# Queries and keys stored by quad and head column, and packed by fewer transfers

## The chip, the core and the metric

The kernel runs on one core of a Trainium2 chip. The metric is the device time of one execution in microseconds; the figure given for a kernel is the median of its runs. Five engines work side by side: PE (TensorE, matrix products), DVE (VectorE), ACT (ScalarE), POOL (GpSimd), and SP (SyncE), which in this kernel issues every DMA transfer. Each engine executes its own instructions strictly in the order in which the program has them; an instruction that waits on a semaphore holds up everything behind it on that engine.

## The reference, cut to what matters

Input `x` is 2048 rows of 640 numbers. Four layers follow one another, each added to its input:

```python
x = x + _A_ref(_layernorm(x))   # attention
x = x + _B_ref(_layernorm(x))   # Fourier mixing
x = x + _A_ref(_layernorm(x))
x = x + _B_ref(_layernorm(x))
```

`_A_ref` makes q, k and v by one 640 x 1920 product, splits them into 32 heads of 20 numbers, takes `q @ k.T * 20 ** -0.5` where the key lies 0 to 255 places behind the query, a softmax over the keys, the product with v, and an output product with a 640 x 640 matrix. `_B_ref` is a two-dimensional DFT by matrix products, of which the real part is kept. Only the two attention layers are touched here.

## The kernel before, in words

Everything is float32. A product of two float32 matrices is made of three products of their halves: a matrix is cut into a rounded upper part ("hi") and the remainder ("lo"), and hi·hi + hi·lo + lo·hi is summed in PSUM (`split` L171, `product3` L182). This holds for q·k too, which matters for the change.

**Projection.** Queries and keys come out transposed, with the feature on the partition and the sequence along the row, in 10 chunks of 128 features by 4 blocks ("sb") of 512 positions. The host has put the columns of the weight in an order in which 160 features in a row belong to one quad (four heads): first 80 of the query, then 80 of the key, and head after head inside these. 160 and 128 don't divide each other, so most chunks hold features of two quads. `piece` (L495) makes one chunk and sb, and `store_qk` (L503) writes hi and lo into the DRAM tensor `qk_d` by one transfer. That is for the first two chunks, before the heads begin; the other eight come from `pieces` (L507) while the heads run, whose `store` (L531) writes hi and lo by a transfer each (L533).

**Heads.** `heads` (L575) is one software pipeline over 128 steps, 16 steps (query blocks of 128) for each of 8 quads. In step `step` the score pass runs for s = step + 10 and the exponent pass for t = step, so that the score pass is 10 steps ahead (`LEAD`):

- score pass (`s_head`, matmul L606): scores of a query block, and on DVE (L611) the mask and the row maximum. Contraction is over 60 partitions: 20 rows of the head three times, queries as hi, lo, hi and keys as hi, hi, lo, so that one matmul makes the three products.
- after every 4 steps `m_rows` (L615) turns the maxima of 512 queries round on PE, ACT writes them negated to the tile `mt` (L622), and two small transfers (L624) put them into partitions 60 and 124 of the query tile `qp`, opposite a row of ones in the key tile `kp`.
- exponent pass (`t_head`, matmul L638): keys against queries over 61 partitions, which subtracts the maximum as well; exponent on ACT (L649), mask on POOL (L655, L659), and the product with v on PE (`pv`, L672).

The first exponent matmul that touches a block's queries needs that block's `mt` rows. For blocks 1 to 3 of a quad it stands a little under three steps behind ACT's write of `mt`; for block 0 two steps more.

**Packing.** `pack` (L557) brings the tiles `kp` and `qp` of a quad from `qk_d`, one block of 512 positions at a time: 20 partitions by two heads by 512 numbers for each of 3 groups of rows, for 2 head pairs, for keys and for queries, so 12 transfers of 80 KB a block (L563). `due` (L710) asks for a block 8 steps before its first use, every 4 steps, and `defer(i // 3, f)` spreads the 12 transfers over four steps, 3 a step. Two sets of `kp` and `qp` alternate by quad.

**Order of the transfers.** All of these stand in SP's one queue in the order in which the Python code reaches them: the packs by step (`defer`), the stores and the small transfers of sums by half step (`post`, `tick`), the loads of v every 4 steps (`load_v` L588), and loads for the output product and the next layer in the last quads. Each transfer counts on one of eight semaphores in turn, and its issue waits until the transfer eight places before it has landed.

Projection matmuls (L204) and later parts of the output product are laid between the heads' matmuls by `share` and `fill` (L740, L757), in numbers fixed when the program is built.

## Time and profile before

| | |
|---|---|
| median of 3 runs | 2169.74 us (2169.26 to 2172.96) |
| profiled execution | 2169.5 us, of which the span of its instructions 2167.7 us |
| PE, DVE, ACT, POOL busy | 97%, 74%, 53%, 43% of the span |
| mean granted PE clock | 0.992 |
| DMA | 222400 packets and 392.26 MB through SP's queue, mean 182 GB/s |
| pack transfers (L563) | 2 x 384 of 80.0 KB |
| heads, first to last exponent matmul | 154.6 to 517 us and 1236.0 to 1595 us |

How to read it: a line such as L638 is a line of the kernel printed above. "PE banks L638 <- DMA qp<-mt" says that PE's matmul of line 638, which writes the tile `banks`, waited for the transfer that wrote `qp` from `mt`. The chain is the path of work that ended last, followed back from the last instruction. Windows give each engine's busy time in a stretch of the span, then the granted PE clock (1.00 is full), the busy share of the 16 DMA engines, and the rate. In a timeline a row is: start, duration, engine ("SPq": SP issuing a transfer), line, operation, tiles, count, and in brackets the idle time before it and what ended that.

### The profile page before, as it was taken

Reading aid. Unit: us, or ns where it says so; the run is one execution under the profiler, and the core shown is the slowest. Engines: PE = TensorE matmul, PEld = TensorE weight load, DVE = VectorE, ACT = ScalarE, POOL = GpSimd, SP = SyncE. Lnnn points to the kernel's source line nnn. Section 1 sums busy time; section 2 is a strip of 40 time slices with the busy share of each in tenths; the row PEclk is TensorE's granted clock in tenths of the full one; section 3 lists DMA queues with packets and bytes.
Section 4 is the critical chain, followed back from the end, with each engine's and each line's share of the span. In section 5 each row is a group of like instructions: output and inputs, shape, how many; then the busy total and the mean of one; then the engine's idle time right before and its main releaser. Section 6 shows DMA issues by size and latency. Waiting matters only on the chain.

```text
span 2167.7 us, 46148 instructions
## 1 busy us (share of the span) xinstructions
PE 2108.8 (97%) x16405; PEld 1749.2 (81%) x16405; DVE 1596.9 (74%) x3936; ACT 1153.9 (53%) x2511; POOL 925.3 (43%) x1455
## 2 busy tenths in 40 slices
PE   8999999999999999999999999999999999999999
PEld 8987776677878888889999877766777788888899
DVE  7358777676897968777751578876778869687777
ACT  3228877666554545543431288776665545455522
POOL 2047776766423234130230487777654323241300
PEclk9999999999999999999999999999999999999999
DMA  6556666786445454757645466667864464546653
GB/s 210 169 162 184 202 191 207 206 229 199 140 125 178 134 180 127 230 193 259 213 143 185 152 186 202 200 205 225 230 183 134 126 189 136 165 149 218 221 177 125
DMA packets 222630, 395.21 MB, mean 182 GB/s; under 512 B 40384, under 2 KB 86976, under 8 KB 222400
## 3 DMA queue, kind: packets, MB, share of 16 engines
q1 hardware_dynamic: 222400, 392.26, 58.3%
q8 instruction: 130, 2.13, 0.4%
q14 instruction: 100, 0.82, 0.1%
HBM read 273.94 MB, written 117.05 MB: 180 GB/s over the span
## 4 chain that ended last, share of the span: by engine, by line
PE 78%; DVE 7%; DMA 5%; ACT 4%; POOL 4%; issue 2%; SPq 1%; ACTq 0%; DVEq 0%; POOLq 0%
PE banks L1373 27%; PE banks L186 15%; PE banks L204 12%; PE banks L672 7%; PE banks L1628 6%; PE banks L638 5%; PE banks L606 4%; DMA qp<-mt 3%; POOL big L179 1%; POOL ou L1303 1%; DVE qp L179 1%; PE banks L286 1%; ACT big L1023 1%; DMA pt<-c 1%; POOL rs L1073 1%
## 5 line engine op out<-in xcount | busy, mean ns | idle before, releaser
L611 DVE CUSTOM_DVE_ANT_0 banks<-banks,mask 128x384 f32<-128x384 f32 (+2 forms) x1024 | 515.0, 566 | 175.5 <-PE banks L606 140.1
L649 ACT ACTIVATE pt<-banks 128x384 f32<-128x384 f32 (+2 forms) x864 | 363.0, 472 | 100.9 <-PE banks L638 47.8
L638 PE MATMUL banks<-qp,kp 61*128 61x384 f32 (+2 forms) x1024 | 336.6, 366 | 19.4 <-DMA qp<-mt 18.2
L606 PE MATMUL banks<-kp,qp 60*128 60x384 f32 (+2 forms) x1024 | 337.4, 370 | 5.4 <-DVE mc L611 4.5
L204 PE MATMUL banks<-big,wc 64*128 64x512 f32 x1920 | 338.4, 398 | 0.4 <-DVE pt L419 0.4
L655 POOL TENSOR_SCALAR_AFFINE_SELECT pt<-pt 128x256 f32<-128x256 f32 x432 | 177.4, 412 | 148.6 <-ACT pt L649 123.8
L638 PEld LDWEIGHTS banks<-qp,kp 61*128 61x128 f32 x1024 | 178.7, 187 | 63.6 <-issue 25.2
L606 PEld LDWEIGHTS banks<-kp,qp 60*128 60x128 f32 x1024 | 174.1, 187 | 58.1 <-DVE mc L611 41.9
L204 PEld LDWEIGHTS banks<-big,wc 64*128 64x128 f32 x1920 | 199.1, 188 | 12.3 <-DVE pt L419 0.5
L1303 POOL TENSOR_TENSOR pt<-pt,pt 128x512 f32<-128x512 f32 x36 | 62.9, 1747 | 289.3 <-DMA pt<-c 176.1
L672 PE MATMUL banks<-pt,vq 128*32 128x128 f32 (+1 forms) x3664 | 178.4, 317 | 1.3 <-POOL pt L655 1.2
L173 ACT ACTIVATE cc<-pt 128x512 fp32r<-128x512 f32 x150 | 94.0, 626 | 155.0 <-POOL pt L1279 52.7
L173 ACT ACTIVATE qp<-pt 128x512 fp32r<-128x512 f32 (+1 forms) x195 | 119.6, 624 | 94.2 <-DVE pt L1304 46.4
L179 DVE TENSOR_TENSOR cc<-pt,cc 128x512 fp32r<-128x512 f32 x150 | 120.1, 811 | 53.5 <-ACT cc L173 51.1
L659 POOL TENSOR_SCALAR_AFFINE_SELECT pt<-pt 128x256 f32<-128x256 f32 x380 | 156.6, 412 | 0.0
L1373 PE MATMUL banks<-qp,big 128*128 128x512 f32 x630 | 151.1, 391 | 5.0 <-DVE qp L179 4.0
L179 DVE TENSOR_TENSOR qp<-pt,qp 128x512 fp32r<-128x512 f32 (+1 forms) x195 | 147.6, 770 | 10.4 <-ACT qp L173 7.7
L672 PEld LDWEIGHTS banks<-pt,vq 128*32 128x32 f32 x3664 | 101.3, 111 | 61.0 <-issue 22.7
L611 DVE DVE_READ_ACCUMULATOR2_ANT mc<- 128x1 f32 x1024 | 146.3, 143 | 0.0
L1373 PEld LDWEIGHTS banks<-qp,big 128*128 128x128 f32 x630 | 117.0, 188 | 31.0 <-DVE qp L179 5.7
L1373 PE MATMUL banks<-qp,xc 128*128 128x512 f32 x480 | 118.0, 391 | 2.0 <-DVE xc L179 1.5
L1373 PEld LDWEIGHTS banks<-qp,xc 128*128 128x128 f32 x480 | 89.8, 188 | 22.6 <-DVE xc L179 2.4
(232 smaller groups left out, 4561.5 us busy)
## 6 DMA issues: line engine op xcount, KB each, us to landing
pt<-c SPq DMA_DIRECT2D x188, 512.0 KB
kp<-qk_d SPq DMA_DIRECT2D x384, 80.0 KB
qp<-qk_d SPq DMA_DIRECT2D x384, 80.0 KB
kp<-u_d SPq DMA_DIRECT2D x32, 640.0 KB
qk_d<-cc SPq DMA_DIRECT2D x64, 256.0 KB
qk_d<-x SPq DMA_DIRECT2D x64, 256.0 KB
o_d<-ou SPq DMA_DIRECT2D x64, 256.0 KB
x_d<-x SPq DMA_DIRECT2D x48, 320.0 KB
```

Of the source, the lines that this page charges most:

```text
L173: nc.scalar.activation(hi, src, AF.Copy, scale=-1.0 if neg else 1.0)
L179: (eng or nc.vector).tensor_tensor(out=lo, in0=src, in1=hi.bitcast(F32), op=OP.subtract)
L186: self.nc.tensor.matmul(p, x, y, start=n == 0, stop=n == last)
L204: self.nc.tensor.matmul(ps[a], x[r], y[r], start=half + i == 0, stop=half == 1 and i == n - 1, skip_group_check=True)
L606: nc.tensor.matmul(p, qp[quad % 2][b:b + 60, z, qb * P:(qb + 1) * P], kp[quad % 2][b:b + 60, z, k0 * P:(qb + 1) * P], start=True, stop=True)
L611: nc.vector.tensor_tensor_reduce(out=p, in0=p, in1=self.mask[:, 384 - n * P:], scale=1.0, scalar=NEG, op0=OP.add, op1=OP.max, accum_out=mc ...
L638: nc.tensor.matmul(self.banks[:, tb[e], :n * P], kp[quad % 2][b:b + 61, z, kb * P:(kb + 1) * P], qp[quad % 2][b:b + 61, z, kb * P:(kb + n) ...
L649: nc.scalar.activation(pt[quad, kb][:, 2 * z + e, :n * P], self.banks[:, tb[e], :n * P], AF.Exp, scale=SCALE)
L655: nc.gpsimd.affine_select(out=t[:, :, 0:P], in_=t[:, :, 0:P], pattern=[[0, 2], [1, P]], compare_op=OP.is_ge, fill=0.0, base=0, channel_mul ...
L659: nc.gpsimd.affine_select(out=t[:, :, 256:384], in_=t[:, :, 256:384], pattern=[[0, 2], [-1, P]], compare_op=OP.is_gt, fill=0.0, base=0, ch ...
L672: nc.tensor.matmul(p[32 * h:32 * h + 32, (c0 - qa) * P:(c1 - qa) * P], vq[:, 96 * (kb % 4) + 21 * h:96 * (kb % 4) + 21 * h + 32], t[:, h, ...
L1373: nc.tensor.matmul(self.banks[:, bk, :], p, b[q], start=start and m == 0, stop=stop and last and m == 2, skip_group_check=True)
```

## The change

`qk_d` becomes a tensor by quad, part (hi, lo), feature of the quad, and position, with rows of 2560 numbers instead of 2048 (512 are never used). The host orders the 160 columns of a quad by feature number first, and by query or key and head after that, so that one head's 20 features lie 8 rows apart, and hi and lo of a head are 40 rows with one step between them. Where two neighbouring groups of the 60 partitions are hi and then lo, one transfer of 40 partitions brings both. `pack` so needs 8 transfers instead of 12, and in the heads it takes two blocks (1024 positions) at once, every 8 steps instead of every 4, spread over six steps. A chunk that holds features of two quads is now stored by two sets of transfers.

```diff
-        self.qk = dram.tile([2, 2 * D, S], F32, name="qk_d")
+        self.qk = dram.tile([NQ, 2, 8 * DH, S + 512], F32, name="qk_d")
...
+    def rows_of(self, c):
+        n, r0, r1 = 8 * DH, c * P, (c + 1) * P
+        for q in range(r0 // n, -(-r1 // n)):
+            a, b = max(r0, q * n), min(r1, q * n + n)
+            yield q, a - q * n, a - r0, b - r0
+
     def store_qk(self, c, sb, st):
-        self.nc.sync.dma_start(
-            self.qk[:, c * P:(c + 1) * P, sb * 512:(sb + 1) * 512].rearrange("l p s -> p l s"), st.bitcast(F32))
+        for q, r0, a, b in self.rows_of(c):
+            self.nc.sync.dma_start(
+                self.qk[q, :, r0:r0 + b - a, sb * 512:(sb + 1) * 512].rearrange("l p s -> p l s"),
+                st[a:b].bitcast(F32))
...
             def store():
-                for l, x in enumerate((hi.bitcast(F32), r)):
-                    self.nc.sync.dma_start(self.qk[l, c * P:(c + 1) * P, sb * 512:(sb + 1) * 512], x)
+                for q, r0, a, b in self.rows_of(c):
+                    for l, x in enumerate((hi.bitcast(F32), r)):
+                        self.nc.sync.dma_start(self.qk[q, l, r0:r0 + b - a, sb * 512:(sb + 1) * 512], x[a:b])
...
-    def pack(self, quad, sb):
+    def pack(self, quad, sb, n=1):
...
-        cols = slice(sb * 512, (sb + 1) * 512)
+        cols = slice(sb * 512, (sb + n) * 512)
...
+        src = self.qk[quad].rearrange("l (r g) s -> (l r) g s", g=8)
         for kind in (1, 0):
             for e in range(2):
-                r0 = 160 * quad + 80 * kind + 40 * e
                 dst = (self.qp, self.kp)[kind][quad % 2].rearrange("p (z s) -> p z s", z=2)
-                for part, l in enumerate(((0, 1, 0), (0, 0, 1))[kind]):
-                    b = 64 * e + 20 * part
-                    src = self.qk[l, r0:r0 + 40, cols].rearrange("(z r) s -> r z s", z=2)
-                    todo.append(lambda d=dst[b:b + 20, :, cols], src=src: put(d, src))
+                g = 4 * kind + 2 * e
+                for part, m in (((0, 2), (2, 1)), ((0, 1), (1, 2)))[kind]:
+                    b = 64 * e + DH * part
+                    todo.append(lambda d=dst[b:b + DH * m, :, cols], src=src[:DH * m, g:g + 2, cols]: put(d, src))
...
-               for q in range(1, NQ) for j in range(NSB)]
+               for q in range(1, NQ) for j in range(0, NSB, 2)]
...
-                for i, f in enumerate(self.pack(q, j)):
-                    defer(i // 3, f)
+                for i, f in enumerate(self.pack(q, j, 2)):
+                    defer(3 * i // 4, f)
...
-        for kind in range(2):
-            for e in range(2):
-                for z in range(2):
-                    b = kind * D + (4 * p + 2 * z + e) * DH
-                    cols.extend(range(b, b + DH))
+        for d in range(DH):
+            for kind in range(2):
+                for e in range(2):
+                    for z in range(2):
+                        cols.append(kind * D + (4 * p + 2 * z + e) * DH + d)
```

On PE, DVE, ACT and POOL the instructions stand in the same order as before, one for one. Only SP's queue differs.

First place: SP in the first attention layer, where the first blocks of quad 3 are packed into `kp_103` and `qp_104` while `mt` rows go to quad 2's `qp_105`. Before:

```order
L563 DMA kp_103<-qk_d 20x2x512 x3
L624 DMA qp_105<-mt 2x4x128 x2
L563 DMA kp_103<-qk_d 20x2x512 x3
L701 DMA r_d<-rc 128x16
L533 DMA qk_d<-cc 128x512
L533 DMA qk_d<-x 128x512
L563 DMA qp_104<-qk_d 20x2x512 x3
L590 DMA vq_90<-v_d 128x384
L563 DMA qp_104<-qk_d 20x2x512 x3
```

Now (the pack is line 572, `mt` line 633, the stores line 542):

```order
L572 DMA kp_103<-qk_d 20x2x1024
L572 DMA kp_103<-qk_d 40x2x1024
L633 DMA qp_105<-mt 2x4x128 x2
L572 DMA kp_103<-qk_d 20x2x1024
L710 DMA r_d<-rc 128x16
L542 DMA qk_d<-cc 128x512
L542 DMA qk_d<-x 128x512
L572 DMA kp_103<-qk_d 40x2x1024
L599 DMA vq_90<-v_d 128x384
L572 DMA qp_104<-qk_d 40x2x1024
L572 DMA qp_104<-qk_d 20x2x1024
```

Two transfers of 160 and 320 KB stand ahead of `mt` where three of 80 KB stood, and 6 transfers in all stand in these rows where 12 did.

Second place: SP four steps later, at the next `mt` rows of the same quad. Before:

```order
L533 DMA qk_d<-cc 128x512
L533 DMA qk_d<-x 128x512
L695 DMA sm<-ou_98 128x1x16
L696 DMA o_d<-ou_98 128x512
L563 DMA kp_103<-qk_d 20x2x512 x3
L624 DMA qp_105<-mt 2x4x128 x2
L563 DMA kp_103<-qk_d 20x2x512 x3
```

Now:

```order
L542 DMA qk_d<-cc 128x512
L542 DMA qk_d<-x 128x512
L704 DMA sm<-ou_98 128x1x16
L705 DMA o_d<-ou_98 128x512
L572 DMA qp_104<-qk_d 40x2x1024
L633 DMA qp_105<-mt 2x4x128 x2
L572 DMA qp_104<-qk_d 20x2x1024
```

One transfer of 320 KB stands ahead of `mt` and one of 160 KB behind it, where three of 80 KB stood on either side; what is now around it is the end of the pack of 1024 positions, where before the next block's pack began here.

Third place: SP's stores of a chunk with features of two quads, early in the heads of the first layer. Before:

```order
L533 DMA qk_d<-cc 128x512
L533 DMA qk_d<-x 128x512
L480 DMA x<-wqk 128x640
L624 DMA qp_105<-mt 2x4x128 x2
L533 DMA qk_d<-cc 128x512
L533 DMA qk_d<-x 128x512
```

Now:

```order
L542 DMA qk_d<-cc 64x512
L542 DMA qk_d<-x 64x512
L542 DMA qk_d<-cc 64x512
L542 DMA qk_d<-x 64x512
L480 DMA x<-wqk 128x640
L633 DMA qp_105<-mt 2x4x128 x2
L542 DMA qk_d<-cc 64x512
L542 DMA qk_d<-x 64x512
L542 DMA qk_d<-cc 64x512
L542 DMA qk_d<-x 64x512
```

Each store of such a chunk is two transfers of half the rows. Over a layer the packs go from 384 transfers to 144, and the stores from 72 to 116.

## The prediction, made before the changed kernel was run

> **What bounds the kernel now.** I read the page first: the span, the busy engines, and the chain of work that ended last.
>
> ```profile
> span 2167.7 us, 46148 instructions
> PE 2108.8 (97%) x16405; PEld 1749.2 (81%) x16405; DVE 1596.9 (74%) x3936; ACT 1153.9 (53%) x2511; POOL 925.3 (43%) x1455
> PE 78%; DVE 7%; DMA 5%; ACT 4%; POOL 4%; issue 2%; SPq 1%; ACTq 0%; DVEq 0%; POOLq 0%
> ```
>
> PE bounds the whole: only 2167.7 - 2108.8 = 58.9 us of its time are idle. The change moves nothing on PE, DVE, ACT or POOL, so all that it can give is idle time of PE and clock lost through it. Next the waits of PE, of the whole span, then of quads 2 to 4 of each attention layer:
>
> ```profile
> PE banks L638 <- DMA qp<-mt: 18.2, 14, 2.6
> ...
> PE banks L638 <- DMA qp<-mt: 5.1, 5, 1.7
> ...
> PE banks L638 <- DMA qp<-mt: 2.9, 3, 1.5
> ```
>
> The largest wait is that of the exponent matmul for the `mt` rows: 14 times, 18.2 us, of which 5.1 + 2.9 = 8.0 us fall into quads 2 to 4 and the other 10.2 into quads 5 and 6. What it costs shows when the span is cut at each quad's first exponent matmul: quads 1 to 6 of layer one, then of layer two.
>
> ```profile
> 195.30:235.60 40.30, 40.30 (x494) 29.66 (x492) 32.88 (x133) 32.81 (x82) 31.34 (x70) 1.00 0.68 202
> 235.60:277.10 41.50, 40.70 (x494) 29.71 (x492) 33.12 (x133) 32.97 (x82) 31.46 (x70) 1.00 0.66 193
> 277.10:320.10 43.00, 40.91 (x496) 29.81 (x494) 33.28 (x133) 32.71 (x83) 31.42 (x70) 1.00 0.67 196
> 320.10:363.30 43.20, 40.97 (x494) 29.75 (x492) 33.21 (x133) 32.97 (x82) 31.44 (x70) 1.00 0.68 200
> 363.30:410.10 46.80, 42.70 (x470) 29.28 (x468) 32.90 (x131) 33.61 (x84) 34.72 (x72) 0.96 0.68 208
> 410.10:470.00 59.90, 55.55 (x732) 41.69 (x730) 41.04 (x152) 35.45 (x89) 41.68 (x78) 0.91 0.78 223
> ...
> 1277.00:1317.30 40.30, 40.30 (x496) 29.61 (x494) 32.87 (x133) 32.82 (x83) 31.40 (x70) 1.00 0.66 200
> 1317.30:1358.60 41.30, 40.68 (x496) 29.65 (x494) 33.15 (x133) 32.94 (x83) 31.42 (x70) 1.00 0.67 199
> 1358.60:1400.50 41.90, 40.92 (x495) 29.71 (x493) 33.19 (x133) 32.86 (x83) 31.42 (x70) 1.00 0.69 202
> 1400.50:1442.70 42.20, 40.73 (x496) 29.71 (x494) 33.16 (x133) 33.07 (x83) 31.44 (x70) 1.00 0.65 198
> 1442.70:1489.60 46.90, 42.28 (x471) 28.71 (x468) 33.06 (x131) 33.83 (x84) 35.06 (x72) 0.96 0.74 220
> 1489.60:1547.80 58.20, 54.35 (x732) 41.37 (x729) 40.19 (x149) 35.46 (x89) 42.11 (x77) 0.91 0.80 224
> ```
>
> Quads 1 to 4 do the same work (494 to 496 matmuls). Quad 1 does it in 40.3 us in both layers, with PE never idle; quads 2 to 4 take longer and longer. Quad 5 has some 24 matmuls fewer and takes 46.8 us. Why is `mt` late? One round of SP's queue, from one pair of `mt` transfers to the next:
>
> ```profile
> 1318.40 1.09 SPq L624 DMA_DIRECT2D qp<-mt  x2
> 1319.64 1.22 SPq L563 DMA_DIRECT2D kp<-qk_d  x3
> 1321.14 0.36 SPq L701 DMA_DIRECT2D r_d<-rc  x1
> 1321.60 0.37 SPq L533 DMA_DIRECT2D qk_d<-cc  x1
> 1322.06 0.38 SPq L533 DMA_DIRECT2D qk_d<-x  x1
> 1322.49 1.33 SPq L563 DMA_DIRECT2D qp<-qk_d  x3
> 1323.92 0.34 SPq L590 DMA_DIRECT2D vq<-v_d  x1
> 1324.31 1.11 SPq L563 DMA_DIRECT2D qp<-qk_d  x3
> 1325.52 0.34 SPq L533 DMA_DIRECT2D qk_d<-cc  x1
> 1326.09 0.34 SPq L533 DMA_DIRECT2D qk_d<-x  x1
> 1326.84 0.60 SPq L695 DMA_DIRECT2D sm<-ou  x1
> 1327.48 0.55 SPq L696 DMA_DIRECT2D o_d<-ou  x1
> 1328.09 1.26 SPq L563 DMA_DIRECT2D kp<-qk_d  x3
> 1329.45 1.14 SPq L624 DMA_DIRECT2D qp<-mt  x2
> ```
>
> 22 transfers are issued in 11.05 us, and the issues alone take 9.3 us of it (the sum of the second column without the last row). A round belongs to four steps, which are worth 40.3 / 4 = 10.1 us when PE isn't held up. So **SP cannot issue a round in the time that PE needs for it**: it falls behind, and `mt` stands behind what is left over. ACT and PE around that last row:
>
> ```profile
> 1325.46 0.25 ACT L622 ACTIVATE mt<-banks 16x128 fp32r<-16x128 f32 x1
> ...
> 1333.08 0.41 PE L638 MATMUL banks<-qp,kp 61*128 61x384 f32 x1 [0.62 <-DMA qp<-mt]
> ```
>
> ACT had `mt` ready at 1325.71. SP issued it 3.74 us later. PE stood ready at 1333.08 - 0.62 = 1332.46 and went on 3.63 us after the issue. The margin is 1332.46 - 1325.71 = 6.75 us, less 3.6 us for the transfer itself: SP may be about 3.1 us late, and here it is 3.7. In quad 0, where the queue isn't yet behind, SP waits for `mt` and not the other way round:
>
> ```profile
> 163.19 0.25 ACT L622 ACTIVATE mt<-banks 16x128 fp32r<-16x128 f32 x1
> ...
> 163.46 1.07 SPq L624 DMA_DIRECT2D qp<-mt  x2
> ```
>
> The Trainium skill's page "DMA: Bandwidth & Descriptors" ("Issuing engines are not separate DMA queues") says that the sequencer's time to initiate a transfer is usually small relative to the transfer. By that rule fewer issues would give nothing and the time would stay (the third rival below). The rows of this round speak against it here.
>
> **The change, part by part.**
>
> *Fewer pack issues.* In two rounds (8 steps, 20.2 us unhindered) 24 pack issues become 8. An issue costs (1.22 + 1.33 + 1.11 + 1.26) / 12 = 0.41 us. No row shows an issue of 40 x 2 x 1024; the bounds are 0.34, the single rows for other tiles, and 0.82, if it grew with the rows of the tile. I take 0.41, since a store of 128 rows (0.37) costs no more than a pack of 40. So 24 x 0.41 = 9.8 us become 8 x 0.41 = 3.3.
>
> *Split stores.* A piece of a chunk with features of two quads has 4 stores instead of 2. Two rounds hold up to 4 pieces, so up to 8 more issues of 0.37 = 3.0 us. The two rounds thus go from 18.6 us to 12.1 us, or 15.1 where chunks are shared, against 20.2: **SP no longer falls behind**, and `mt` waits for at most what stands just ahead of it, 2 or 3 issues of some 1.2 us in all, inside the 3.1.
>
> *What that gives.* Quads 2 to 4 go back to quad 1's 40.3 us: 41.5 + 43.0 + 43.2 + 41.3 + 41.9 + 42.2 = 253.1, less 6 x 40.3 = 241.8, is 11.3 us. In quads 5 and 6 the waits for `mt` are 10.2 us. Two of the longest of them are followed within 2 us by a stretch at half clock (a matmul that waited, and the window after it, of each):
>
> ```profile
> 371.40 0.41 PE L638 MATMUL banks<-qp,kp 61*128 61x384 f32 x1 [2.58 <-DMA qp<-mt]
> ...
> 371.80:375.20 3.40, 3.40 (x26) 2.40 (x28) 2.39 (x9) 1.96 (x4) 0.99 (x3) 0.50 0.83 257
> ...
> 1527.11 0.41 PE L638 MATMUL banks<-qp,kp 61*128 61x384 f32 x1 [2.00 <-DMA qp<-mt]
> ...
> 1528.90:1532.30 3.40, 3.40 (x39) 2.27 (x37) 1.31 (x7) 1.34 (x4) 1.28 (x4) 0.50 0.66 208
> ```
>
> Each is 3.4 us at a granted clock of 0.50, worth 1.7 us: 3.4 us in all. That makes 13.6 us in quads 5 and 6. I count 10.2 of it, midway between half and all. There POOL is busy 34.7 of 46.8 and 41.7 of 59.9 us, and quad 6 has a clock of 0.91, more than one such stretch explains, so other waits will partly step in.
>
> *Larger transfers.* The bytes are the same: 24 x 80 KB are 4 x 160 + 4 x 320 KB. But 480 KB now go out ahead of every second `mt` where it was 240; at the 193 to 202 GB/s of the rows above that is 2.4 us of traffic and not 1.2, most of it gone in the step (2.5 us) between. Bounds for one `mt`: 0 and 1.2 us later, inside the margin once SP is on time; I take 0 for the sum.
>
> *At nothing.* In the stretch before the heads, 48 packs become 32 and 4 stores are added; PE works there on the projection and value products, far ahead of the packs. If that cover were gone, each issue more or less would be worth 0.4 us: 12 x 0.4 = 5 us a layer in the change's favour. The row step of 10 KB and the hi/lo order in DRAM I take at nothing too: the pieces are 4 KB instead of 2, with the same number of bytes. If the new layout slowed the packs, the slower rival below would show it.
>
> Sum: 11.3 + 10.2 = 21.5 us. The profiled execution took 2169.5 us (1.8 outside its span), the median of the runs is 2169.74, so they can stand for each other. 2169.5 - 21.5 = **2148 us, the forecast.**
>
> **The rivals.**
>
> 1. *The wait shrinks but stays.* SP is on time, but `mt` lands late behind the 480 KB. For it: this transfer's own 3.6 us are more than half the margin. Against: quad 1 has packs ahead of its `mt` rows too, and PE isn't idle there. Half of 21.5 is left: 2169.5 - 10.7 = 2159.
> 2. *More comes free.* Quad 5 also reaches 40.3 (6.5 + 6.6 = 13.1), and quad 6 loses its idle time (59.9 - 55.55 + 58.2 - 54.35 = 8.2) and half its lost clock, 0.09 x 118 / 2 = 5.3, as the loads behind the packs in the queue come sooner too. With 11.3 that is 37.9: 2132.
> 3. *No change.* SP's lateness isn't the number of issues but the waits inside its queue (stores for POOL, sums for ACT), which remain: 2169. Against: the gaps between the issues are 11.05 - 9.3 = 1.8 us of a round.
> 4. *Slower.* SP stays late, and every second `mt`, behind 480 KB, lands 1.2 us later. It decides once SP's lateness there is over 3.1 - 1.2 = 1.9 us. 28 of the 56 `mt` pairs of quads 1 to 7 stand so. If SP stays as late as in the row above (3.7), about 3.7 + 1.2 - 3.1 = 1.8 us are waited 28 times instead of 18.2 us in all: 50 - 18 = 32 us more at worst, a third of that with the rest on time: 2180. For it: the slow growth of the lateness, and up to 8 issues more by split stores. Against: 16 issues fewer.
>
> The Trainium skill's same page, under "Why a DMA increments its semaphore by 16 and not by 1", says that a transfer uses the largest number of DMA engines up to 16 that divides the slowest dimension of both sides. For 20 rows and for 40 rows that is ten. By this, as an estimate, 480 KB would take 16/10 as long as on all sixteen, in the sense of rivals 1 and 4; no row here shows the engines apart, and before and after it would be ten alike.
>
> **How the numbers follow.** Forecast 0.65, rival 1 0.16, rival 2 0.07, rival 3 0.06, rival 4 0.06. The forecast's own range is 2169.5 less 11.3 + 6.8 to 11.3 + 13.6, with 3 us either way for where clock stretches fall: 2142 to 2154. To leave out no more than 2 in 10, the range reaches to rival 2 and over rival 1: 2132 to 2164. What can be told from no change is 0.2%, 4.3 us. Faster by more: 0.65 + 0.16 + 0.07, less 0.02 for a rival 1 that ends short: 0.86. Within: 0.08. Slower: 0.06.
>
> **What would show it.** Right: the wait L638 <- `qp<-mt` falls from 18.2 us to under 4; quads 2 to 4 take 40.3 to 40.8 us; SP issues `mt` within 2 us of ACT's write; the two clock stretches are gone. Wrong: SP's issue of a 40-row pack takes much over 0.41 us; `mt` takes over 5 us to land; quads 2 to 4 stay over 41.5 us though SP is on time; or new waits for `qp<-qk_d` or `kp<-qk_d` appear.

## The result

| | median | range | profiled execution |
|---|---|---|---|
| before | 2171.35 us | 2169.26 to 2172.97 | 2169.5 us |
| changed | 2222.99 us | 2219.35 to 2225.38 (4 runs) | 2221.65 us |

The ratio is 1.0237, with an interval of 1.0218 to 1.0256: the change makes the kernel **slower by about 52 us**. The forecast was 2148 us, faster. It had the wrong sign, and the time lies outside its range.

First the page of the changed kernel: span, PE, and the chain that ended last, by engine and by line. In it the score matmul is L615 (L606 before), the exponent matmul L647 (L638), the pack L572 (L563), the transfer of `mt` L633 (L624).

```profile
span 2219.9 us, 45701 instructions
PE 2129.3 (96%) x16405; PEld 1761.4 (79%) x16405; DVE 1599.7 (72%) x3936; ACT 1154.8 (52%) x2511; POOL 930.8 (42%) x1455
...
PE 73%; DMA 11%; DVE 6%; POOL 4%; ACT 3%; issue 2%; SPq 1%; POOLq 0%; DVEq 0%; ACTq 0%
PE banks L1382 28%; PE banks L186 15%; PE banks L204 10%; DMA qp<-qk_d 7%; PE banks L1637 6%; PE banks L681 6%; PE banks L615 3%; PE banks L647 3%; POOL big L179 1%; DVE banks L620 1%; DMA r_d<-rc 1%; PE banks L286 1%; ACT big L1032 1%; DVE qp L179 1%; POOL ou L1312 1%
```

PE's idle time is 2219.9 - 2129.3 = 90.6 us, where it was 58.9: 31.7 us more. The other 20.5 of the 52.2 us that the span has grown are busy time: the same 16405 matmuls at a lower clock. The mean granted clock went from 0.992 to 0.981, and the trace's clock records show 21 stretches at half clock, 85 us in all, where they showed 10 with 37 us. On the chain, DMA has grown from 5% to 11%, and 7% of the span is a transfer that isn't among the lines of the chain that the page of before lists: `qp<-qk_d`, the pack itself. There `qp<-mt` stood with 3%.

PE's waits in the changed kernel, over the span (total, times, longest):

```profile
PE banks L615 <- DMA qp<-qk_d: 23.5, 15, 2.7
PE banks L647 <- DMA qp<-mt: 10.4, 9, 2.1
...
PE banks L615 <- DMA r_d<-rc: 3.8, 4, 2.2
...
PE banks L615 <- DMA o_d<-ou: 3.1, 1, 3.1
PE banks L615 <- DMA x<-wqk: 2.9, 1, 2.9
```

The wait for `mt` has fallen from 18.2 to 10.4 us. In its place **the score matmul waits for its pack**, which before it never did. The waits named `r_d`, `o_d` and `x` belong to it too: L615 reads nothing of these tiles, and at every block start PE goes on 0.09 to 0.28 us after the block's last pack has landed (the landings are read below). The name is that of another transfer.

The quads (windows from first to first exponent matmul; quads 1 to 6 of layer one, quads 1 to 4 of layer two, and at the end quad 0 of both layers, before and now; the columns are PE, PE's loads, DVE, ACT, POOL, the granted clock, the busy share of the DMA engines, GB/s):

```profile
198.80:244.70 45.90, 42.48 (x496) 30.61 (x494) 33.31 (x133) 32.85 (x83) 31.52 (x70) 0.96 0.64 183
244.70:289.30 44.60, 40.98 (x496) 29.79 (x494) 33.17 (x133) 32.80 (x83) 31.54 (x70) 1.00 0.69 188
289.30:339.40 50.10, 45.07 (x494) 32.15 (x492) 33.36 (x133) 33.17 (x82) 31.51 (x70) 0.90 0.62 167
339.40:388.70 49.30, 43.88 (x496) 31.71 (x494) 33.39 (x133) 33.14 (x83) 31.49 (x70) 0.93 0.66 183
388.70:435.20 46.50, 43.12 (x471) 29.68 (x468) 32.94 (x131) 33.79 (x84) 34.87 (x72) 0.93 0.70 193
435.20:493.70 58.50, 54.44 (x730) 41.83 (x727) 40.24 (x149) 35.46 (x89) 43.11 (x78) 0.91 0.86 225
...
1305.10:1350.10 45.00, 42.31 (x494) 30.33 (x492) 33.17 (x133) 32.84 (x82) 31.55 (x70) 0.96 0.67 186
1350.10:1397.60 47.50, 43.53 (x496) 31.23 (x494) 33.32 (x133) 33.04 (x83) 31.53 (x70) 0.93 0.65 177
1397.60:1446.20 48.60, 44.02 (x494) 31.27 (x492) 33.32 (x133) 33.02 (x82) 31.51 (x70) 0.93 0.65 173
1446.20:1493.50 47.30, 42.56 (x495) 30.86 (x493) 33.32 (x133) 33.02 (x83) 31.50 (x70) 0.96 0.68 189
...
154.60:195.30 40.70, 40.55 (x455) 29.80 (x455) 33.18 (x133) 32.14 (x81) 31.63 (x71) 0.96 0.62 190
1236.00:1277.00 41.00, 40.77 (x457) 29.82 (x457) 33.20 (x133) 32.15 (x81) 31.59 (x71) 0.96 0.61 188
...
154.60:198.80 44.20, 41.33 (x457) 29.93 (x457) 33.49 (x133) 32.24 (x81) 31.77 (x71) 0.96 0.69 191
1259.60:1305.10 45.50, 43.03 (x456) 31.23 (x456) 33.35 (x133) 32.45 (x81) 31.76 (x71) 0.92 0.65 185
```

Quads 1 to 4, which took 40.3 to 43.2 us, now take 44.6 to 50.1: 44.6 us more in the two layers together. The rest of the loss, 3.5 and 4.5 us, lies in quad 0, in which the score pass, 10 steps ahead, already opens quad 1. Quads 5 and 6 have hardly changed. In quads 1 to 4 the rate of the DMA engines is lower, not higher.

SP's timeline ahead of one such wait, in quad 1:

```profile
214.50 1.16 SPq L572 DMA_DIRECT2D kp<-qk_d  x2
219.17 1.10 SPq L633 DMA_DIRECT2D qp<-mt  x2
220.32 0.42 SPq L572 DMA_DIRECT2D kp<-qk_d  x1
...
222.19 0.36 SPq L572 DMA_DIRECT2D kp<-qk_d  x1
...
223.38 0.86 SPq L572 DMA_DIRECT2D qp<-qk_d  x2
...
228.06 0.29 SPq L572 DMA_DIRECT2D qp<-qk_d  x1
229.32 2.29 SPq L633 DMA_DIRECT2D qp<-mt  x2
231.72 0.35 SPq L572 DMA_DIRECT2D qp<-qk_d  x1
```

SP is on time at the first of these two `mt`: from 215.66 to 219.17 it has nothing to do but wait for ACT's write. But the eight packs of this block go out from 214.50 to 231.72, and the last one stands behind the second `mt`. PE, and a window after it:

```profile
238.34 0.41 PE L615 MATMUL banks<-kp,qp 60*128 60x384 f32 x1 [2.17 <-DMA r_d<-rc]
...
238.80:242.20 3.40, 3.40 (x32) 2.25 (x32) 2.37 (x9) 1.15 (x3) 1.37 (x3) 0.51 0.42 134
```

PE was ready for this block at 238.34 - 2.17 = 236.17, which is 4.45 us after the last pack was issued. It went on 6.62 us after that issue. Then come 3.4 us at a clock of 0.51.

The same reading for every block of the pipeline, from the landings of the packs (medians; "spare" is the median of the time from the landing of the block's last pack to PE being ready for it; "late" counts the blocks whose pack came after that; "idle" is what PE waited at the blocks' first score matmuls, in sum; in e9 the pack is that of the first 512 positions). The rows after the second are experiments told below.

```
kernel                    blocks  last issue  last pack   spare   late  idle
                                  to PE ready lands in    us            us
before                        56       8.3       4.1       4.1      0    0.2
changed                       28       4.3       5.2      -1.0     28   40.5
e2  512 a block, early        56      10.6       4.6       5.7      0    0.4
e8  512 a block, late         56       5.2       3.2       1.9      8    6.0
e3  1024 a block, early       28       9.7       7.8       2.2      0    0.0
e9  1024 in pieces, late      28       3.3       3.9      -0.6     23   27.4
e11 1024, last before mt      28       6.6       7.3      -0.1     14   17.6
e12 1024, early, no split     28      10.2       8.3       2.1      1    1.0
e7  512, early, no split      56      11.5       4.8       6.7      0    0.4
```

In the changed kernel **the last pack of all 28 blocks is late**. The 40.5 us at their starts, less the 7.8 us that the waits for `mt` gave back, make 32.7 us, and PE is idle 31.7 us more than before.

The waits for `mt` that are left follow the packs too. The same records of blocks 1 and 3 of a quad, which have no pack beside them, show the second `mt` transfer issued 0.6 us after ACT's write and landed 1.6 us later. At blocks 0 and 2, which have one, it is issued 2.3 and 3.1 us after the write and lands 5.1 and 4.3 us later (medians). Block 0 has two steps more; all nine waits for `mt`, the 10.4 us, stand at block 2.

### The profile page after: what moved, and what is told of

The parts are those of the page before. It is cut to its first block, busy times and chain, and to the rows that moved or that the text cites. A ratio compares the mean times of both kernels' runs of the same rounds, so it can differ in the third digit from the quotient of the medians.

```text
span 2219.9 us, 45701 instructions
## 1 busy us (share of the span) xinstructions
PE 2129.3 (96%) x16405; PEld 1761.4 (79%) x16405; DVE 1599.7 (72%) x3936; ACT 1154.8 (52%) x2511; POOL 930.8 (42%) x1455
## 4 chain that ended last, share of the span: by engine, by line
PE 73%; DMA 11%; DVE 6%; POOL 4%; ACT 3%; issue 2%; SPq 1%; POOLq 0%; DVEq 0%; ACTq 0%
PE banks L1382 28%; PE banks L186 15%; PE banks L204 10%; DMA qp<-qk_d 7%; PE banks L1637 6%; PE banks L681 6%; PE banks L615 3%; PE banks L647 3%; POOL big L179 1%; DVE banks L620 1%; DMA r_d<-rc 1%; PE banks L286 1%; ACT big L1032 1%; DVE qp L179 1%; POOL ou L1312 1%
## 5 line engine op out<-in xcount | busy, mean ns | idle before, releaser
L615 PE MATMUL banks<-kp,qp 60*128 60x384 f32 (+2 forms) x1024 | 339.6, 374 | 45.8 <-DMA qp<-qk_d 23.5
L647 PE MATMUL banks<-qp,kp 61*128 61x384 f32 (+2 forms) x1024 | 340.7, 369 | 11.8 <-DMA qp<-mt 10.4
L204 PE MATMUL banks<-big,wc 64*128 64x512 f32 x1920 | 346.8, 405 | 0.4 <-DVE pt L419 0.4
L615 PEld LDWEIGHTS banks<-kp,qp 60*128 60x128 f32 x1024 | 177.5, 191 | 101.4 <-DVE mc L620 49.3
L647 PEld LDWEIGHTS banks<-qp,kp 61*128 61x128 f32 x1024 | 182.9, 191 | 55.3 <-ACT pt L658 20.1
L204 PEld LDWEIGHTS banks<-big,wc 64*128 64x128 f32 x1920 | 203.8, 191 | 12.1 <-DVE pt L419 0.5
L681 PE MATMUL banks<-pt,vq 128*32 128x128 f32 (+1 forms) x3664 | 184.4, 328 | 0.6 <-POOL pt L664 0.6
L179 DVE TENSOR_TENSOR qp<-pt,qp 128x512 fp32r<-128x512 f32 (+1 forms) x195 | 156.7, 816 | 10.5 <-ACT qp L173 7.9
L179 DVE TENSOR_TENSOR cc<-pt,cc 128x512 fp32r<-128x512 f32 x150 | 120.0, 810 | 50.1 <-ACT cc L173 47.9
L1382 PEld LDWEIGHTS banks<-qp,big 128*128 128x128 f32 x630 | 117.0, 188 | 31.1 <-DVE qp L179 5.7
```

Source lines behind the costliest of these rows:

```text
L179: (eng or nc.vector).tensor_tensor(out=lo, in0=src, in1=hi.bitcast(F32), op=OP.subtract)
L204: self.nc.tensor.matmul(ps[a], x[r], y[r], start=half + i == 0, stop=half == 1 and i == n - 1, skip_group_check=True)
L615: nc.tensor.matmul(p, qp[quad % 2][b:b + 60, z, qb * P:(qb + 1) * P], kp[quad % 2][b:b + 60, z, k0 * P:(qb + 1) * P], start=True, stop=True)
L647: nc.tensor.matmul(self.banks[:, tb[e], :n * P], kp[quad % 2][b:b + 61, z, kb * P:(kb + 1) * P], qp[quad % 2][b:b + 61, z, kb * P:(kb + n) ...
L681: nc.tensor.matmul(p[32 * h:32 * h + 32, (c0 - qa) * P:(c1 - qa) * P], vq[:, 96 * (kb % 4) + 21 * h:96 * (kb % 4) + 21 * h + 32], t[:, h, ...
L1382: nc.tensor.matmul(self.banks[:, bk, :], p, b[q], start=start and m == 0, stop=stop and last and m == 2, skip_group_check=True)
```

## The experiments

The theory after the result: the block's last transfers are issued too late (step 5 of 8, where it was step 3) and take longer to land in a burst of two blocks' packs. The rivals: the new layout itself (its row step, or 4 KB pieces); the split stores; the eight places of SP's queue; the ten DMA engines that a pack uses.

| | edit | median | ratio to before |
|---|---|---|---|
| e1 | layout and stores as changed, packs as before | 2187.96 | 1.0094 (1.0075 to 1.0113) |
| e2 | changed, blocks of 512, two transfers a step | 2146.64 | 0.9913 (0.9891 to 0.9935) |
| e3 | changed, two transfers a step | 2168.42 | 1.0007 (0.9994 to 1.0021) |
| e4 | changed, packs cut to 16 or 32 rows and a rest | 2292.97 | 1.0571 (1.0545 to 1.0597) |
| e5 | changed, row step of 8 KB | 2222.48 | 1.0265 (1.0244 to 1.0286) |
| e6 | old layout, blocks of 1024, 12 transfers | 2197.36 | 1.0132 (1.0085 to 1.0180) |
| e7 | e2 without split stores | 2138.14 | 0.9876 (0.9854 to 0.9897) |
| e8 | e2, the transfers spread as in the change | 2152.01 | 0.9942 (0.9922 to 0.9962) |
| e9 | changed, each pack as two of 512 | 2211.11 | 1.0191 (1.0176 to 1.0206) |
| e10 | e1 without split stores | 2164.61 | 0.9980 (0.9968 to 0.9993) |
| e11 | changed, last pack ahead of `mt` | 2211.96 | 1.0216 (1.0190 to 1.0242) |
| e12 | e7 with blocks of 1024 | 2153.04 | 0.9933 (0.9909 to 0.9957) |

### The layout and the stores alone

e1 keeps the layout and the split stores of the change, and packs as before: 12 transfers of 20 rows by 512, three a step.

```diff
-                for part, m in (((0, 2), (2, 1)), ((0, 1), (1, 2)))[kind]:
+                for part, l in enumerate(((0, 1, 0), (0, 0, 1))[kind]):
...
-                for i, f in enumerate(self.pack(q, j, 2)):
-                    defer(3 * i // 4, f)
+                for i, f in enumerate(self.pack(q, j)):
+                    defer(i // 3, f)
```

> The new layout and its split stores, but the packs as before the change: 12 transfers of 20 rows by 512 positions a block, every 4 steps, 3 a step. Theory (large packs on ten DMA engines come too late): 2 KB packets on the ten engines go at the old pace, landing in 3.3 to 3.8 us, no waits of the score matmul for a pack; the split stores load SP's queue a little more, so 2168 to 2185 us. Rival 1 (the layout makes reading slow, rows 80 KB apart): over 2195 us, packs landing in 5 us or more.

2187.96 us, just above what was expected: 20 us slower than before (2167.56 beside it). The waits of e1, then of e10 (below), which differs from it in the split stores alone:

```profile
PE banks L647 <- DMA qp<-mt: 31.1, 15, 4.1
```

```profile
PE banks L644 <- DMA qp<-mt: 12.0, 10, 2.9
```

`mt` waits 31.1 us where it was 18.2: with 12 packs a block, the extra stores push SP further behind. No score matmul waits for a pack. So the layout with its split stores costs something, but not what the change lost, and by another wait.

### Blocks of 512

e2 is the change without its larger blocks: 8 transfers, of 512 positions, every 4 steps, two a step.

```diff
-               for q in range(1, NQ) for j in range(0, NSB, 2)]
+               for q in range(1, NQ) for j in range(NSB)]
...
-                for i, f in enumerate(self.pack(q, j, 2)):
-                    defer(3 * i // 4, f)
+                for i, f in enumerate(self.pack(q, j)):
+                    defer(i // 2, f)
```

> The change with its merged transfers of 40 rows, but 512 positions at a time, every 4 steps, 2 transfers a step (the last at step 3 of 8). Theory: half the bytes in a burst and two steps more for the last one; SP has 16 issues where 24 were, mt waits under 5 us, no waits for packs: 2145 to 2160 us. Rival 1 (layout): over 2190. Rival 2 (only the issue of the last transfer at step 5 is too late): 2145 to 2160 too, so this run alone doesn't part it from the theory.

2146.64 us, faster than before by 0.9%, and 76 us faster than the change. PE's wait for `mt` and quads 1 to 4 of layer one:

```profile
PE banks L647 <- DMA qp<-mt: 3.8, 3, 1.7
```

```profile
195.80:236.10 40.30, 40.30 (x496) 29.58 (x494) 32.86 (x133) 32.79 (x83) 31.39 (x70) 1.00 0.69 208
236.10:276.40 40.30, 40.30 (x496) 29.56 (x494) 32.86 (x133) 32.78 (x83) 31.39 (x70) 1.00 0.68 207
276.40:316.70 40.30, 40.30 (x496) 29.56 (x494) 32.86 (x133) 32.78 (x83) 31.37 (x70) 1.00 0.70 198
316.70:357.10 40.40, 40.40 (x494) 29.61 (x492) 32.88 (x133) 32.86 (x82) 31.37 (x70) 1.00 0.71 206
```

This is the profile that the prediction described: quads at 40.3 us, `mt` waits under 4. Packing hi and lo by one transfer does what it was forecast to do; what loses the time is bringing two blocks at once, spread as it is. The next two runs take these two apart.

### Size and spread apart

e3 leaves the blocks at 1024 and issues the packs earlier, the last at step 3:

```diff
-                    defer(3 * i // 4, f)
+                    defer(i // 2, f)
```

> The change with 1024 positions, its 8 transfers issued 2 a step over four steps instead of over six: the last one two steps (5 us) earlier. Theory: the waits of the score matmul for packs fall from some 36 us to under 8, but the burst is denser, 1.9 MB in 10 us on ten engines, and small transfers stand behind it: the mt waits grow from 10 us to 20 or more; 2180 to 2205 us. Rival 2 (only the late issue): 2145 to 2160, mt waits no longer than 10 us. Rival 1 (layout): over 2200.

2168.42 us, better than the theory expected: 55 us of the loss are gone by this line alone. PE doesn't wait at a block's start (idle 0.0), but it waits again for `mt`:

```profile
PE banks L647 <- DMA qp<-mt: 17.1, 14, 3.0
```

e8 is the other half: blocks of 512 as in e2, spread as in the change.

```diff
-                    defer(i // 2, f)
+                    defer(3 * i // 4, f)
```

> The run with blocks of 512 and merged transfers, but the 8 transfers spread over six steps as in the change, so that the last is issued at step 5 of 8. Theory (late issue costs only together with the long landing of the large packs): a pack lands in some 4.5 us and has 7.6, so no waits for packs: 2143 to 2156 us. Rival (the late issue alone): waits for packs of 20 us or more, over 2180.

2152.01 us, 5 us over e2, with intervals that overlap. Set against each other, by spare time in the table of block starts and by median:

| | last at step 3 | last at step 5 |
|---|---|---|
| 512 | 5.7 us, 2146.64 | 1.9 us, 2152.01 |
| 1024 | 2.2 us, 2168.42 | -1.0 us, 2222.99 |

Either edit takes 3 to 4 us of the spare time, and neither alone uses it up (e8 comes near: 8 of its 56 blocks are late). **Both together do**, and the time jumps by 49 us more than the two single losses (5 and 22) make. The late spread takes it by issuing later (10.6 to 5.2, 9.7 to 4.3), the larger block by landing later (4.6 to 7.8, 3.2 to 5.2).

### Packet size, row step, old layout

e9 issues each transfer of the change as two of 512, at the same steps: the same bytes and burst, in pieces of 2 KB again.

```diff
-                for i, f in enumerate(self.pack(q, j, 2)):
-                    defer(3 * i // 4, f)
+                for i, f in enumerate(zip(self.pack(q, j), self.pack(q, j + 1))):
+                    for g in f:
+                        defer(3 * i // 4, g)
```

> The change's own schedule (1024 positions every 8 steps, over six steps), but each of its 8 transfers made as two of 512 positions, issued one behind the other: the same bytes at the same places in the queue, in 2 KB packets, with 16 pack issues in 8 steps instead of 8. Theory A (the amount in a burst is what costs): packs still land in 6 to 7 us, waits for packs of 20 us or more, 2195 to 2225 us. Theory B (4 KB packets are what costs, because the ten engines move them more slowly under load): packets at a median near 84 ns, packs landing in 4 to 5 us, waits for packs under 6 us, 2145 to 2165.

2211.11 us. The transfers are those of e8, one for one in size and number; only that two blocks stand together. Still it is 59 us slower than e8:

```profile
PE banks L615 <- DMA qp<-qk_d: 21.4, 17, 2.8
PE banks L647 <- DMA qp<-mt: 13.9, 10, 2.3
```

So 4 KB pieces are not the main cause; two blocks at once are. In e9 the last pack is issued 3.3 us before PE is ready, where e8 has 5.2, and takes 3.9 us to land, where e8 has 3.2. By the trace's packet records a single 4 KB packet does take longer in the burst: the median is 159 ns in the Fourier layers, and 204 and 208 ns in the change's packs of the two attention layers (2 KB: 84 ns). But taking it away gives back only 12 us.

e5 takes away the 512 unused numbers of a row in DRAM.

```diff
-        self.qk = dram.tile([NQ, 2, 8 * DH, S + 512], F32, name="qk_d")
+        self.qk = dram.tile([NQ, 2, 8 * DH, S], F32, name="qk_d")
```

> The change with DRAM rows of 2048 numbers instead of 2560, so that the rows of one head lie 64 KB apart instead of 80. Theory (what costs is the size of the packs and their late issue): the same as the change within 6 us, 2217 to 2229, 4 KB packets at a median near 204 ns as there. Rival (the step between rows slows the reads of 4 KB): their median moves by 20 ns or more and the time by 10 us or more, either way.

2222.48 us, as the change: the row step has no part in the loss.

e6 is the kernel before with blocks of 1024: 12 transfers of 20 rows every 8 steps, three a step, the last at step 3.

```diff
-               for q in range(1, NQ) for j in range(NSB)]
+               for q in range(1, NQ) for j in range(0, NSB, 2)]
...
-                for i, f in enumerate(self.pack(q, j)):
+                for i, f in enumerate(self.pack(q, j, 2)):
                     defer(i // 3, f)
```

> The kernel before with its own layout and its 12 transfers of 20 rows, but 1024 positions at a time, every 8 steps, 3 a step over four steps: SP has 12 pack issues in 8 steps where 24 were, and no split stores. Theory (blocks of 1024 fill the ten engines for long, whatever the layout): 4 KB packets at a median over 190 ns, mt waits 12 us or more, 2155 to 2175 us, like the run with the packs earlier. Rival (the new layout makes the 4 KB packets slow): median near 159 ns, mt waits under 8 us, 2140 to 2155.

2197.36 us, above what was expected of it, though it halves the pack issues and has no split stores. So fewer issues are no gain by themselves:

```profile
PE banks L638 <- DMA qp<-mt: 29.3, 13, 4.7
...
PE banks L606 <- DMA qp<-qk_d: 3.9, 1, 3.9
```

The wait for `mt` grows from 18.2 to 29.3 us. SP's waits for earlier transfers to land (all rows of that kind, between 195 and 400 us) are 17.2 us before and 53.4 here; 38.5 in the change, 47.4 in e3 and 19.1 in e2. Blocks of 1024 hold the eight places longer: that is how SP is late with larger transfers, though it issues fewer. In e6 it issues the second `mt` transfer 3.6 and 5.2 us after ACT's write at blocks 0 and 2, where a pack stands beside it, and 0.6 us after at blocks 1 and 3.

### The last pack ahead of `mt`

```diff
-                    defer(3 * i // 4, f)
+                    defer((0, 0, 1, 2, 3, 3, 4, 4)[i], f)
```

> The change with one thing moved: the last of a block's 8 transfers stands ahead of the mt pair of that step in SP's queue and not behind it. In the change's trace the score matmul that opens each block goes on 0.09 us after the block's last transfer has landed, at all 28 blocks, and PE idles 40.5 us there; that transfer is issued 5.4 us before, since SP waits first for mt and for free places. Theory (issued late times lands late): it is issued some 2.5 us earlier, the idle time at the block starts falls from 40 to under 12 us, the time to 2170 to 2195; mt waits grow a little, to 10 to 18 us. Rival (the ten engines are full, so whatever stands last lands as late): 2210 or more, the idle time still over 30 us.

2211.96 us, between what was expected of the two ways. The idle time at block starts falls from 40.5 to 17.6 us, but now `mt` pays:

```profile
PE banks L647 <- DMA qp<-mt: 24.9, 13, 3.6
PE banks L615 <- DMA qp<-qk_d: 9.1, 7, 2.6
```

The order of these two in the queue mostly settles which of them is late. The last pack has 2.3 us more until PE is ready, and takes 2.1 us longer to land.

### All DMA engines

The trace's semaphore updates show how many engines a transfer uses, and so answer what the prediction left open: a pack of 20 or of 40 rows has one update just behind its issue (0.1 to 0.4 us) and ten as it lands, a transfer of 128 rows sixteen as it lands, `mt` (2 rows) one and two. So packs run on ten engines, before and after. By the Trainium skill's page "DMA: Bandwidth & Descriptors" ("Why a DMA increments its semaphore by 16 and not by 1"), each engine that a transfer uses adds one update as its data land, and 20 or 40 rows use ten. The trace agrees with its ten updates. e4 cuts each pack into 32 + 8 or 16 + 4 rows, so that the first part uses all sixteen.

```diff
+                    for r0, r1 in ((0, 16 * m), (16 * m, DH * m)):
+                        todo.append(lambda d=dst[b + r0:b + r1, :, cols], src=src[r0:r1, g:g + 2, cols]: put(d, src))
...
-                    defer(3 * i // 4, f)
+                    defer(3 * i // 8, f)
```

> The change with each pack transfer cut in two, of 16 or 32 rows and of the 4 or 8 left over, spread over the same six steps: 16 transfers in 8 steps, and the larger ones can run on sixteen DMA engines. Theory: packs land in 4 us instead of 7, waits for packs under 8 us, mt waits under 8; SP's load is between that of before and of the change; 2148 to 2170 us. Rival 1 (layout): rows as far apart, so still over 2195. Rival 2 (late issue): the last transfer is still issued at step 5, so over 2195 as well.

2292.97 us, far worse than expected:

```profile
PE banks L616 <- DMA qp<-qk_d: 41.7, 16, 5.7
PE banks L648 <- DMA qp<-mt: 24.9, 12, 3.5
PE banks L616 <- DMA r_d<-rc: 17.8, 5, 10.3
```

The first parts show 16 updates, so the edit did what it says. But there are twice as many transfers for the eight places (PE is ready 2.3 us after the last issue, not 4.3), the rests run on 8 and 4 engines, and a 4 KB packet takes a median of 287 ns in layer one and 268 in layer two. e9 has as many transfers and is 82 us faster, so their number isn't the whole of it. The parts of 32 rows, on sixteen engines, land in 4.7 us (keys) and 6.0 (queries); the change's 40 rows, on ten, in 5.6 and 7.4 (medians). That is four fifths of the bytes in about four fifths of the time, so no gain by the engines shows here. As more transfers stand beside them in e4, whether ten engines limit a pack stays open.

### Without split stores

e7 deals the features otherwise. The first 128 of a quad's 160 are a chunk of its own, and the last 32 of four quads make one more chunk, so that no chunk is split by two sets of transfers; the rest is e2's.

```diff
-                for q, r0, a, b in self.rows_of(c):
-                    for l, x in enumerate((hi.bitcast(F32), r)):
-                        self.nc.sync.dma_start(self.qk[q, l, r0:r0 + b - a, sb * 512:(sb + 1) * 512], x[a:b])
+                for l, x in enumerate((hi.bitcast(F32), r)):
+                    self.nc.sync.dma_start(self.place(c, l, slice(sb * 512, (sb + 1) * 512)), x)
...
+    def place(self, c, l, cols):
+        if c in (1, 6):
+            t = 4 * (c // 6)
+            return self.qk[t:t + 4, l, P:8 * DH, cols].rearrange("q r s -> r q s")
+        return self.qk[c - (c > 1) - (c > 6), l, :P, cols]
```

> The blocks of 512 with merged transfers (8 a block, 2 a step), and the features dealt to the chunks so that no chunk is shared: eight chunks of 128 features of one quad, two of the last 32 of four quads, each stored by two transfers. Theory (SP's issues set the time while transfers are small): 5 to 9 issues fewer a quad than in the run with blocks of 512, mt waits under 3 us, quads 5 and 6 shorter: 2136 to 2146 us. Rival (with mt waits at 3.8 us nothing is left to take): 2145 to 2150.

2138.14 us, ratio 0.9876 (0.9854 to 0.9897): **faster than both kernels**, 27 us below the one before (2165.14 beside it) and 85 below the change. Quads 1 to 6 of layer one:

```profile
195.40:235.60 40.20, 40.20 (x494) 29.59 (x492) 32.79 (x133) 32.79 (x82) 31.45 (x70) 1.00 0.68 208
...
316.20:356.50 40.30, 40.30 (x496) 29.70 (x494) 32.90 (x133) 32.87 (x83) 31.46 (x70) 1.00 0.71 217
356.50:398.80 42.30, 40.75 (x470) 28.11 (x468) 32.61 (x131) 33.47 (x84) 34.80 (x72) 1.00 0.73 224
398.80:451.60 52.80, 50.17 (x732) 38.67 (x730) 40.09 (x149) 35.29 (x89) 42.98 (x79) 1.00 0.86 243
```

The last two quads gain as well: 42.3 and 52.8 us, where before they took 46.8 and 59.9. Among PE's waits none for `mt` is listed any more.

e10 is e7 with the 12 packs of before, three a step.

> The layout and the unshared chunks of the run without split stores, but with the packs as before the change (12 of 20 rows by 512, 3 a step): SP issues what it issued before, only from another layout. Theory (the 20 us that the layout alone cost were the split stores' issues): like the kernel before, 2160 to 2172 us, mt waits 15 to 21 us. Rival (the layout itself costs by its reads): 2178 or more.

2164.61 us, 0.9980 (0.9968 to 0.9993): the layout, its stores unshared, is worth nothing or a few us. So e1's 20 us are the split stores, and 22 to 26 us (e10 to e7, by the ratios and by the medians) are what hi and lo by one transfer gives.

e12 is e7 with blocks of 1024 every 8 steps, still two transfers a step.

> The run without split stores (blocks of 512, unshared chunks), with blocks of 1024 instead, 2 transfers a step over four steps: half the pack issues, the same bytes, each burst twice as large. Theory (large packs hold mt and the eight places in flight, even when they are early enough): mt waits 10 us or more where that run has hardly any, 2152 to 2170 us, slower than blocks of 512. Rival (fewer issues always pay once the packs come early and no store is split): 2138 or less.

2153.04 us, 15 us slower than e7. PE waits at neither place for long, and less for `mt` than the 10 us that were expected:

```profile
PE banks L644 <- DMA qp<-mt: 4.8, 9, 0.9
```

So the larger block, which halves the pack issues once more, isn't a gain even with the best spread seen here. The Trainium skill's page "DMA: Bandwidth & Descriptors" ("Rules for kernel authors") advises to coalesce many small transfers into one large one, above all below 64 KB. Here that holds where two packs of 80 KB become one of 160 (e10 to e7) and a round of SP was full. From packs of 80 and 160 KB to packs of 160 and 320 (e7 to e12) the runs go against it.

## Why the prediction was wrong

*What bounds the kernel, and why `mt` was late: right.* SP could not issue a round in the time that PE needs for it. With fewer issues and the same block (e2), `mt` is on time and the waits for it fall from 18.2 to 3.8 us.

*Fewer pack issues: right in price.* The trace of the changed kernel, L572, in ns (least, median, most):

```profile
L572 SPq DMA_DIRECT2D kp<-qk_d x144: 273/360/1098, 43.6 to 1572.8; - x144
L572 SPq DMA_DIRECT2D qp<-qk_d x144: 273/344/1554, 45.3 to 1586.1; - x144
```

The median issue of a pack is 0.34 to 0.36 us (112 of each 144 are of 1024 positions); 0.41 was taken. By size the medians are 0.34 us for 80 KB before, 0.37 to 0.39 for 160 and 0.30 to 0.36 for 320 in the change, so the issue of a pack doesn't grow with its bytes.

*Split stores: too cheap.* They were counted as at most 3.0 us of SP's time in two rounds, at 0.37 us each, and as room that was there anyway. In the trace of the change a store of 64 rows takes SP 0.59 us to issue (median of 64), one of 32 or 96 rows 0.40 to 0.42, where one of 128 took 0.37 before; four pieces so add 3.6 to 6.4 us. Why 64 rows take longest, no run shows. e2 against e7 shows 8.5 us for the kernel where SP has room, e1 against e10 some 20 to 23 where it has none.

*What that gives: right, for another kernel.* Quads 1 to 4 at 40.3 us and 2148 us as a whole were forecast; e2 measured 40.3 to 40.4 in layer one, and 2146.64. The steps up to here describe e2. That its time comes within 2 us of the forecast is partly luck: its split stores still cost the 8.5 us, which the sum had at nothing, so the rest gives more than the sum's 21.5.

*Larger transfers: this step failed.* "Bounds for one `mt`: 0 and 1.2 us later, inside the margin once SP is on time; I take 0 for the sum." It asked only what the 480 KB do to `mt`, and not when the pack itself is needed. The profile of before had this margin: from a block's last pack to its first score matmul 8.3 us, of which the landing takes 4.1. The spread over six steps (`3 * i // 4` in place of `i // 3`) moves the last issue two steps back, some 5 us: that alone is more than the 4.1 us of spare time, with the landing as before (e8, where SP issues sooner, keeps 1.9). In the changed kernel PE is ready 4.3 us after the last issue, and the landing takes 5.2. The price was 40.5 us of idle time at 28 starts and with it most of the 20.5 us of lost clock, where 0 was taken. The 0 for `mt` itself was too low as well, though far less so: behind its pack it lands in 4.3 to 5.1 us instead of 1.6, and 10.4 us of waits are left, where under 4 were forecast.

*At nothing: right for the row step* (e5: no difference) and, with e10, for the hi/lo order.

*The rivals.* The fourth had the side right, and of the mechanism the smaller part: every second `mt` is indeed issued and landed late, but the waits for it fell to 10.4 us, and the loss came from the pack, which this rival doesn't name. Its 2180 us lie 43 us below the result. "New waits for `qp<-qk_d`" stood among the signs of a wrong prediction, without a place or price; it should have been a rival, since the step of the last issue could be read from the change.

*What is shown and what is argued.* That spread and size are both needed for the loss, and that row step and (but for 12 us) packet size aren't, is shown by e2, e3, e8, e9 and e5. That in a burst transfers are issued later for want of places is argued from SP's waits, and that they land later by the traffic beside them from the landing times; what limits that traffic, the ten engines or something else, no run separates. That the lost clock comes from the idle times is argued from their order in time (below). The time of e12 over e7 isn't traced to one wait.

## What to carry to other kernels

For every transfer that is moved or made larger, work out its own due time first: from its issue to its first reader, less the time to land, with the landing priced for its new size and for what is issued beside it. Fewer and larger transfers relieve a full issuing queue, but they bunch the traffic and hold the queue's places longer; merge until the queue keeps pace, and test each step beyond that. Two edits that each use up half of a margin look harmless one by one, so test them together.

## What the runs showed of the hardware

- A short idle time of PE can cost more than itself. The starts of 28 blocks cost PE 1.45 us each (40.5 / 28), and the span grew by 20.5 us of busy time besides; one wait of 2.17 us is followed by 3.4 us at a clock of 0.51 (above). In the heads of the changed kernel 11 of the 13 idle times of 1.5 us or more have a stretch at half clock within 3.5 us (2 of 5 before), and 6 of the 52 of 0.3 to 1.0 us have one. The Trainium skill's page "TensorE: Matmul & The Clock Gate" ("Why this matters for your kernels") names idle gaps of over about 3 us as what to avoid. Here gaps of 2 us already came with a window of half clock.
- SP issues a pack of 320 KB as fast as one of 80 KB (0.30 to 0.36 us and 0.34, medians), but a store of 64 rows and 128 KB takes it 0.59. Larger packs then let it wait longer for earlier landings: 38.5 us between 195 and 400 us in the change, 19.1 in e2.
- A transfer of 4 KB lands in 1.6 us where no pack stands beside it, and in 4.3 to 5.1 us behind one of 1024 positions (`mt` in the change, medians).
- More engines for a transfer brought no gain: 32 rows on sixteen engines landed in 4.7 and 6.0 us, 40 rows on ten in 5.6 and 7.4, in step with their bytes, and the kernel lost another 70 us (e4).
